# First keys in four loads, first key sketches in one wide buffer, a and b loaded behind the values, and a new order of the opening

## The chip, the cores and the metric

The kernel runs on one core of a Trainium2 chip. The metric is device time in microseconds of one execution; lower is better. The core has five engines that run their own instruction streams and wait for each other through semaphores: PE (matrix multiply, with weight loads shown apart as PEld), DVE (vector), ACT (scalar, with activation functions), POOL (used here for small set-up work) and SP (issues loads and stores). Loads and stores can be issued on SP's queue or on ACT's; in the profile SP's is q1 and ACT's q10, and the packets of both run on 16 DMA engines.

## The reference

Four batches of four heads with 1088 tokens of width 32 go through a linear attention with a polynomial sketch of rank 8, and the result through a dense layer with a rational activation.

```python
def phi(x):                                   # [b, h, s, 32] -> [b, h, s, 64]
    a = np.einsum('rd,bhsd->bhsr', S1, x)
    b = np.einsum('rd,bhsd->bhsr', S2, x)
    return np.einsum('bhsi,bhsj->bhsij', a, b).reshape(*x.shape[:-1], r * r)
q_p, k_p = phi(q), phi(k)
kv = np.einsum('bhsf,bhsd->bhfd', k_p, v)
z = np.sum(k_p, axis=2)
num = np.einsum('bhsf,bhfd->bhsd', q_p, kv)
den = np.einsum('bhsf,bhf->bhs', q_p, z)[..., None] + 1e-06
x = (num / den)                               # -> [4352, 128]
h = x @ w_in                                  # [4352, 2048]
P = a[0] + a[1]*h + a[2]*h**2 + a[3]*h**3
Q = 1.0 + abs(b[0])*abs(h) + abs(b[1])*h**2
return (P / (Q + 1e-06)) @ w_out              # [4352, 128]
```

## The kernel before

**Keys.** Tokens are laid out so that a partition holds 34 tokens of one head (4 heads x 32 groups). They are seen as `NM` = 4 runs m of `NT` = 9 tiles t, of which the last run has only `NL` = 7 (W = 288 floats to a run). DVE transposes blocks of them into `kT` (`kt0` to `kt3`, L250), PE multiplies with the two sketch matrices (`ks`, L256), ACT copies the second half of the sketches out of PSUM (`kc`, L263), DVE forms their outer product with the first half (`kf`, L268), and PE multiplies with the values (`kp`, L297), adding up over all tiles. ACT then copies the sums into `kvz` (`kk`, L307). For the first batch there are three parts of sketches (tiles 0 and 1, 2 and 3, 4 to 8) and four blocks of transposes: kt0 and kt1 take two tiles of all four runs, kt2 tiles 4 to 8 of three runs, kt3 tiles 4 to 6 of the fourth.

**Queries.** For each block of tokens: transpose (`qt`, L320, DVE), sketches (`qs`, L333, PE), copy (`qc`, ACT), features (`qf`, DVE), products with kvz (`qp`, L360, PE), division (`qd`, `qi`, `qx`), transpose back on PE (`qb`) and copy into `xT` (`qk`, L390, ACT). The first two blocks (0 and 1) use a wide PSUM buffer for their sketches. Later blocks of each batch send their sketches through DRAM to spread them over the partitions (class `Spread`).

**The dense layer.** Tokens go in units of 256 or 512. Hidden matmuls (`h`, L446) fill a wide buffer of two PSUM banks, ACT casts it to bfloat16 (`e`, L452), DVE forms the denominator (`u`, `w`, `y`), ACT takes its inverse through a logarithm and an exponential (`ln`, `ex`), DVE forms the numerator's terms (`s`, `m`, `x`, and `pa` on ACT or `pd` on DVE), and PE gathers the output (`G`, L579). The output weights are loaded in two halves (`lw`), scaled by a[0] and a[1] or only cast, and kept in bfloat16 in six pieces (`wo`, L612 to L616; ACT makes 0, 1, 3 and 5, DVE makes 2 and 4).

**Order.** The string `ORDER` is the program's order: each token is a step and an index, and each engine runs its own instructions in that order. Loads are steps too: `lw` output weights, `lq` queries, `lx` input weights, `lk` keys, `lv` values; for index 0, `lq` is the second part of the first batch's queries. `tn` runs matmuls on zeros whose result nobody reads; `TURNS` gives their number: tn:0 has 10, tn:1 and tn:4 have 2 each. `ba` takes the absolute value of b.

**Buffers.** PSUM has two wide buffers (`wide`, 1024 floats, two banks) and four single banks (`bank`). The wide ones serve, in the order of the program, the first keys' sketches, the first two query blocks, and then the hidden matmuls. A new tile takes a buffer whose last reader stands earlier in the order, and its first writer waits for that reader. `kT` has one buffer, features of keys have two, transposed queries (`qT`) two.

**The first loads.** SP issues the sketch matrix S2, the first four tiles of all four runs of keys (256 KB), the first half of the queries, and the values in four loads; ACT issues S1, the rest of the keys (240 and 48 KB), a and b, and loads its activation table. The steps of ORDER follow on SP.

Of the kernel before, what the change touches and what calls it, by code (L numbers as in the profile page):

```python
# [20 lines left out]
ORDER = """
tn:4 tn:0 lw:1 kt0:0 lq:0 kt2:0 lw:0 kt3:0 lx:1 kt1:0 ks0:0 lk:1 qt:0 ks2:0 kc0:0 lx:0 kf0:0 ba:0 qt:1 tn:1 kc2:0 qs:0
kf2:0 qc:0 kp0:0 qf:0 ks1:0 qs:1 kc1:0 kf1:0 qc:1 kp1:0 wo:1 qt:3 kp2:0 qf:1 qt:2 qs:3 kk:0 lq:1 wo:4 lv:1 qp:0 wo:0
qs:2 qd:0 qc:2 qi:0 qx:0 wo:5 qf:2 qb:0 qp:1 qk:0 qc:3 wo:3 h2:0 qd:1 qi:1 qx:1 kt0:1 h3:0 wo:2 e2:0 qt:5 qt:4 qp:2
kt1:1 e3:0 h1:0 pa1:0 u1:0 w1:0 h0:0 y1:0 qd:2 e1:0 qi:2 qx:2 qs:4 e0:0 qb:1 qb:2 qt:6 ks1:1 qk:1 u0:0 qk:2 ln1:0 w0:0
ks0:1 y0:0 h1:1 kc1:1 ex1:0 kf1:1 lk:2 h3:1 lq:2 e1:1 s1:0 kc0:1 h0:1 e3:1 kf0:1 pa0:0 m1:0 h2:1 qf:3 e0:1 x1:0 qp:3
qc:4 e2:1 kt0:2 h0:2 ln0:0 u1:1 kt1:2 h1:2 w1:1 e0:2 ex0:0 y1:1 ks0:2 h2:2 e1:2 s0:0 qd:3 ln0:1 h3:2 qi:3 m0:0 e2:2
lk:3 qx:3 kp1:1 x0:0 e3:2 ex0:1 u1:2 qb:3 lv:2 G0:0 pd0:1 qk:3 w1:2 ln1:1 G1:0 G2:0 qf:4 G3:0 kc0:2 kk:1 y1:2 ex1:1
G4:0 G5:0 kf0:2 qp:4 ln0:2 s0:1 qs:5 G0:1 qd:4 qc:5 qi:4 ex0:2 qt:7 G1:1 qx:4 m0:1 qb:4 ks1:2 qk:4 s1:1 pa1:1 h2:3
s0:2 kc1:2 m1:1 h3:3 e2:3 kf1:2 h1:3 e3:3 st:0 x1:1 ln1:2 qs:7 x0:1 h0:3 e1:3 kt1:3 m0:2 h2:4 e0:3 pd1:2 pa0:2 u1:3  # L30
h3:4 qt:9 w1:3 e2:4 G2:1 ex1:2 x0:2 h0:4 qf:5 e3:4 kp1:2 s1:2 pa0:3 y1:3 h1:4 qc:7 e0:4 m1:2 ln0:3 qp:5 kt0:3 e1:4
G3:1 x1:2 ex0:3 G4:1 m0:3 G5:1 u1:4 ks0:3 qd:5 ln1:3 qi:5 G0:2 w1:4 G1:2 pa1:3 qx:5 G2:2 y1:4 lv:3 qb:5 G3:2 qk:5
ex1:3 h0:5 m1:3 v0:3 kk:2 ln0:4 h2:5 s1:3 e0:5 qs:6 G4:2 qf:7 ex0:4 h1:5 x0:3 qt:8 qc:6 e2:5 s0:4 e1:5 h3:5 pd0:4
# [35 lines left out]
def kernel(  # L69
# [161 lines left out]
    class Keys:  # L231
        def __init__(self, b, k_sb, v_sb, first=False):
            self.b, self.dst, self.k_sb, self.v_sb = b, kvz[b % 2], k_sb, v_sb
            self.take = wide if first else bank
# [16 lines left out]

        def sketches(self, part):
            t0, n = self.PARTS[part]
            ab = self.ab[part] = self.take()[:, 0:n * H * 2 * R].rearrange("p (t h s r) -> p t h s r", h=H, s=2, r=R)
            for t in range(t0, t0 + n):
                nc.tensor.matmul(ab[:, t - t0].rearrange("p h s r -> p (h s r)"),  # L256
                                 lhsT=self.kT[:, t * 128:(t + 1) * 128],
                                 rhs=S12.rearrange("p h s r -> p (h s r)"), start=True, stop=True)
# [450 lines left out]
```

## Time and profile before

| | us |
|---|---|
| median of 3 runs | 274.24 |
| lowest and highest | 274.19, 274.42 |
| time of the profiled execution | 274.34 |
| its span on the core | 272.6 |
| first transpose of keys (L250) starts | 5.84 |
| first sketches of keys (L256) start | 6.34 |
| first hidden matmuls (L446) start | 18.82 |

| stretch, us | PE busy | DVE busy | ACT busy | DMA share |
|---|---|---|---|---|
| 0 to 5.84 | 4.65 | 0.92 | 1.28 | 0.56 |
| 262 to 272.6 | 4.76 | 5.30 | 2.83 | 0.34 |

Busy time is in us; the three stretches between stand with the prediction. The DMA share is the mean busy share of the 16 engines, and it can pass 1 because packets overlap. An instruction's start is in us from the span's start. A wait is named by what ended it. PE's busy time in the first stretch is the matmuls on zeros.

### The profile page before, as it was taken

The page shows a single profiled execution, that of the slowest core. Times are in us where ns is not written, and L with a number is a line of the kernel's source. Part 1 is how long each engine was busy: PE and PEld are TensorE (multiplying, and loading weights), DVE is VectorE, ACT ScalarE, POOL GpSimd, SP SyncE. Part 2 cuts the span into 40 slices and gives each one's busy share as a digit, 9 for nine tenths or more (in the row PEclk, how much of TensorE's full clock was granted, in tenths as well). Part 3 has the DMA queues.
Part 4 walks back from the last instruction along what each step waited for, and adds up shares of the span by engine and source line. Part 5 has one row for each costly group of instructions (what it writes and reads, how often), then busy time and mean ns, then how long its engine had stood idle before and what let it go on. Part 6 is the DMA issues. An engine that isn't in the chain of part 4 may idle for free.

```text
span 272.6 us, 3564 instructions
## 1 busy us (share of the span) xinstructions
PE 258.3 (95%) x1318; PEld 135.4 (50%) x1318; DVE 255.9 (94%) x276; ACT 250.0 (92%) x224; POOL 2.9 (1%) x24
## 2 busy tenths in 40 slices
PE   7989999999999899999999999999999999989591
PEld 3778656963564354535454554434544443434230
DVE  2858999999999999999999999999999999999992
ACT  1377999998999999999999999999999999999980
POOL 4000000000000000000000000000000000000000
PEclk9999999999999999999999999999999999999999
DMA  6992607314025062222304000300126100020005
GB/s 166 294 336 80 204 14 173 111 55 95 2 84 129 14 140 77 73 71 39 96 6 117 11 1 6 120 6 0 23 88 96 20 0 0 0 41 1 0 0 77
DMA packets 30465, 19.53 MB, mean 72 GB/s; under 512 B 20337, under 2 KB 26609, under 8 KB 30449
## 3 DMA queue, kind: packets, MB, share of 16 engines
q1 hardware_dynamic: 28416, 18.87, 26.7%
q10 hardware_dynamic: 2032, 0.45, 0.9%
q8 instruction: 10, 0.16, 0.3%
q14 instruction: 7, 0.05, 0.1%
HBM read 16.16 MB, written 3.15 MB: 71 GB/s over the span
## 4 chain that ended last, share of the span: by engine, by line
PE 37%; ACT 28%; DVE 22%; issue 7%; DMA 2%; SPq 1%; DVEq 0%; ACTq 0%
PE h_ps L446 18%; PE att_ps L579 9%; ACT hh L452 8%; ACT ln L537 8%; ACT r L541 7%; ACT p L532 4%; DVE g L549 4%; DVE s L545 4%; DVE w L486 4%; PE att_ps L360 3%; DVE g L560 3%; DVE w L481 2%; DVE u L475 2%; DMA k_sb<-in_k_dram 2%; PE att_ps L297 1%
## 5 line engine op out<-in xcount | busy, mean ns | idle before, releaser
L446 PE MATMUL h_ps<-xT,w_in_sb 128*128 128x512 f32 (+1 forms) x288 | 125.4, 577 | 1.3 <-ACT hh L452 1.1
L446 PEld LDWEIGHTS h_ps<-xT,w_in_sb 128*128 128x128 f32 x288 | 52.2, 190 | 55.9 <-issue 40.5
L452 ACT CAST hh<-h_ps 128x1024 bf16<-128x1024 f32 x68 | 68.3, 1025 | 3.4 <-PE h_ps L446 2.9
L541 ACT ACTIVATE r<-ln 128x2048 bf16<-128x2048 f32 (+1 forms) x35 | 66.0, 1886 | 0.3
L537 ACT ACTIVATE ln<-w 128x2048 f32<-128x2048 bf16 (+1 forms) x35 | 66.0, 1885 | 0.2
L579 PEld LDWEIGHTS <-w_out 128*128 128x128 bf16 x412 | 39.9, 98 | 52.8 <-issue 18.7
L532 ACT ACTIVATE p<-hh,a_sb 128x2048 bf16<-128x2048 bf16 (+1 forms) x23 | 46.7, 2036 | 0.1
L545 DVE TENSOR_TENSOR s<-hh,r 128x2048 bf16<-128x2048 bf16 (+2 forms) x33 | 40.7, 1241 | 0.2
L486 DVE TENSOR_TENSOR w<-w,u 128x4096 bf16<-128x4096 bf16 (+2 forms) x22 | 39.5, 1795 | 0.1
L579 PE MATMUL att_ps<-g,w_out 128*128 128x512 bf16 (+1 forms) x144 | 34.9, 367 | 4.0 <-DVE g L560 3.8
L579 PE MATMUL att_ps<-r,w_out 128*128 128x512 bf16 (+1 forms) x144 | 34.5, 367 | 0.8 <-ACT r L541 0.8
L549 DVE TENSOR_TENSOR g<-hh,s 128x2048 bf16<-128x2048 bf16 (+1 forms) x30 | 35.1, 1172 | 0.0
L560 DVE TENSOR_TENSOR g<-g,p 128x2048 bf16<-128x2048 bf16 (+1 forms) x30 | 34.8, 1173 | 0.0
L579 PE MATMUL att_ps<-s,w_out 128*128 128x512 bf16 (+1 forms) x124 | 30.0, 365 | 0.0
L481 DVE TENSOR_SCALAR w<-u,b_abs 128x4096 bf16<-128x4096 bf16 (+2 forms) x22 | 23.8, 1090 | 0.1
L475 DVE TENSOR_SCALAR u<-hh 128x4096 uint16<-128x4096 uint16 (+2 forms) x22 | 21.3, 970 | 0.6 <-ACT hh L452 0.2
L360 PEld LDWEIGHTS att_ps<-kvz,q_pT 128*128 128x128 f32 x144 | 17.6, 191 | 5.0 <-DVE q_pT L424 1.1
L360 PE MATMUL att_ps<-kvz,q_pT 128*128 128x66 f32 x144 | 17.9, 273 | 0.9 <-DVE q_pT L352 0.5
L297 PEld LDWEIGHTS att_ps<-v_sb,k_p 128*64 128x64 f32 (+1 forms) x288 | 8.8, 138 | 2.6 <-issue 1.8
L527 DVE TENSOR_SCALAR p<-hh,a_sb 128x2048 bf16<-128x2048 bf16 x12 | 9.6, 804 | 0.0
L297 PE MATMUL att_ps<-v_sb,k_p 128*64 128x64 f32 (+1 forms) x288 | 9.5, 224 | 0.0
L424 DVE TENSOR_TENSOR q_pT<-a_all,b_all 128x768 f32<-128x768 f32 (+1 forms) x10 | 8.9, 895 | 0.0
(60 smaller groups left out, 134.9 us busy)
## 6 DMA issues: line engine op xcount, KB each, us to landing
a_all<-sk_d SPq DMA_DIRECT2D x6, 384.0 KB
b_all<-sk_d SPq DMA_DIRECT2D x12, 192.0 KB
v_sb<-in_v_dram SPq DMA_DIRECT2D x12, 144.0 KB
k_sb<-in_k_dram SPq DMA_DIRECT2D x3, 544.0 KB
q_sb<-in_q_dram SPq DMA_DIRECT2D x3, 544.0 KB
a_all<-sk_d SPq DMA_DIRECT2D x4, 320.0 KB
b_all<-sk_d SPq DMA_DIRECT2D x8, 160.0 KB
out_dram<-out_sb SPq DMA_DIRECT2D x18, 64.0 KB
```

Source lines behind the costliest of these rows:

```text
L360: nc.tensor.matmul(self.nd[:, o:o + 2 * KW], lhsT=self.q_p[:, c, x:x + 128], rhs=kvz[self.b % 2][:, c, :], start=True, stop=True)
L446: nc.tensor.matmul(t[:, x * tl:(x + 1) * tl], lhsT=w_in_sb[:, f * 128:(f + 1) * 128], rhs=xT[:, t0:t0 + tl], start=True, stop=True)
L452: nc.scalar.copy(out=live[i]["hh"][:, part * PW:(part + 1) * PW], in_=live[i]["h", part])
L481: nc.vector.tensor_scalar(out=t[:, c], in0=live[i]["u"][:, c], scalar1=ab1, scalar2=ab0, op0=AX.mult, op1=AX.add)
L486: nc.vector.tensor_mul(out=t[:, c], in0=t[:, c], in1=live[i]["u"][:, c])
L532: nc.scalar.activation(out=part_of(i, "p", h), in_=hh, func=ACT.Identity, scale=a3, bias=a2)
L537: nc.scalar.activation(out=t, in_=live[i]["w"][:, span(h)], func=ACT.Ln, bias=1.0 + 1e-6)
L541: nc.scalar.activation(out=part_of(i, "r", h), in_=live[i]["ln"], func=ACT.Exp, scale=-1.0)
L545: nc.vector.tensor_mul(out=part_of(i, "s", h), in0=hh, in1=part_of(i, "r", h))
L549: nc.vector.tensor_mul(out=part_of(i, "g", h), in0=hh, in1=part_of(i, "p" if horner(i, first(h)) else "s", h))
L560: nc.vector.tensor_mul(out=g, in0=g, in1=part_of(i, "s" if horner(i, first(h)) else "p", h))
L579: nc.tensor.matmul(outs[t0][:, :tl], lhsT=w_sb[y][:, f0 + x, :], rhs=part_of(i, key, h)[:, c:c + tl], start=done[0] == 0, stop=done[0] == ...
```

## The change

Computation and instructions of the compute engines are the same; only loads, buffers and order differ.

- The first batch's keys come in four loads. For the first four tiles, and then for tiles 4 to 8, SP's queue takes runs 0 and 1 and ACT's queue runs 2 and 3. The last load is rectangular, so it also reads two tokens past the end of the fourth run (into padding that nothing reads). Before, it was one load on SP and two on ACT.
- a and b are loaded on SP, behind the values, not on ACT.
- All three parts of the first key sketches lie in one wide buffer, at columns 0, 128 and 512; before, each part took a wide buffer of its own.
- ORDER is another permutation of the same 725 steps. In the opening: all 14 matmuls on zeros stand before the first sketches (tn:1 was between ks2 and qs0); PE's order is ks0, ks1, qs0, ks2, kp0, qs1 where it was ks0, ks2, tn:1, qs0, kp0, ks1, qs1; lx:0 stands before lk:1; ba stands behind kk; the pieces wo change places; in the second batch's start DVE runs kt1:1, kt0:1, qt:6, qt:4 and later qt:5, where it ran kt0:1, wo:2, qt:5, qt:4, kt1:1 and later qt:6. Further on some neighbours swap places, the last of them at step 545.
- `LX`, which nothing reads, goes from 2 to 3.

```diff
-    nc.sync.dma_start(out=k0.rearrange("p (m x) -> p m x", m=NM)[:, :, 0:4 * D],
-                      in_=bass.AP(tensor=k.tensor, offset=k.offset, ap=[[S * D // 32, 128], [W, NM], [1, 4 * D]]))
-    nc.scalar.dma_start(out=k0[:, 0:km].rearrange("p (m x) -> p m x", m=NM - 1)[:, :, 4 * D:],
-                        in_=k0_src[:, 0:km].rearrange("p (m x) -> p m x", m=NM - 1)[:, :, 4 * D:])
-    nc.scalar.dma_start(out=k0[:, km + 4 * D:S], in_=k0_src[:, km + 4 * D:S])
+    half, row = NM // 2, S * D // 32
+    for t0, t1 in ((0, 4), (4, NT)):
+        for x, queue in enumerate((nc.sync, nc.scalar)):
+            at = x * half * W + t0 * D
+            queue.dma_start(out=k0.rearrange("p (m x) -> p m x", m=NM)[:, x * half:(x + 1) * half, t0 * D:t1 * D],
+                            in_=bass.AP(tensor=k.tensor, offset=k.offset + at, ap=[[row, 128], [W, half], [1, (t1 - t0) * D]]))
...
-    nc.scalar.dma_start(out=a_sb, in_=bass.AP(tensor=moe_a.tensor, offset=moe_a.offset,
-                                              ap=[[0, 128]] + list(moe_a.ap)))
-    nc.scalar.dma_start(out=b_sb, in_=bass.AP(tensor=moe_b.tensor, offset=moe_b.offset,
-                                              ap=[[0, 128]] + list(moe_b.ap)))
     nc.scalar.preload_act_table_set("natural_log_exp_and_others")
     load_v(0)
+    nc.sync.dma_start(out=a_sb, in_=bass.AP(tensor=moe_a.tensor, offset=moe_a.offset,
+                                            ap=[[0, 128]] + list(moe_a.ap)))
+    nc.sync.dma_start(out=b_sb, in_=bass.AP(tensor=moe_b.tensor, offset=moe_b.offset,
+                                            ap=[[0, 128]] + list(moe_b.ap)))
...
         def sketches(self, part):
             t0, n = self.PARTS[part]
-            ab = self.ab[part] = self.take()[:, 0:n * H * 2 * R].rearrange("p (t h s r) -> p t h s r", h=H, s=2, r=R)
+            if self.first:
+                if not self.ab:
+                    self.all = wide()
+                at = (0, 128, 512)[part]
+            else:
+                self.all, at = bank(), 0
+            ab = self.ab[part] = self.all[:, at:at + n * H * 2 * R].rearrange("p (t h s r) -> p t h s r", h=H, s=2, r=R)
```

The opening of ORDER, before and after:

```diff
-tn:4 tn:0 lw:1 kt0:0 lq:0 kt2:0 lw:0 kt3:0 lx:1 kt1:0 ks0:0 lk:1 qt:0 ks2:0 kc0:0 lx:0 kf0:0 ba:0 qt:1 tn:1 kc2:0 qs:0
-kf2:0 qc:0 kp0:0 qf:0 ks1:0 qs:1 kc1:0 kf1:0 qc:1 kp1:0 wo:1 qt:3 kp2:0 qf:1 qt:2 qs:3 kk:0 lq:1 wo:4 lv:1 qp:0 wo:0
-qs:2 qd:0 qc:2 qi:0 qx:0 wo:5 qf:2 qb:0 qp:1 qk:0 qc:3 wo:3 h2:0 qd:1 qi:1 qx:1 kt0:1 h3:0 wo:2 e2:0 qt:5 qt:4 qp:2
+tn:1 tn:0 kt0:0 kt1:0 kt3:0 lw:1 kt2:0 tn:4 lq:0 ks0:0 qt:0 lw:0 ks1:0 qt:1 kc0:0 lx:1 qs:0 kf0:0 kc1:0 lx:0 kf1:0
+lk:1 qc:0 ks2:0 qf:0 kp0:0 kc2:0 qs:1 kf2:0 qc:1 kp1:0 wo:1 qf:1 kp2:0 qt:3 qt:2 qs:3 kk:0 lq:1 qp:0 lv:1 ba:0 wo:3
+qs:2 qd:0 qc:2 qi:0 qx:0 wo:0 qf:2 qb:0 qp:1 wo:4 qk:0 qc:3 wo:5 h2:0 qd:1 qi:1 wo:2 qx:1 h3:0 e2:0 kt1:1 kt0:1 qp:2
```

More of the change, by code (lines that the diff above doesn't have):

```diff
@@ L21 @@
 ORDER = """
-tn:4 tn:0 lw:1 kt0:0 lq:0 kt2:0 lw:0 kt3:0 lx:1 kt1:0 ks0:0 lk:1 qt:0 ks2:0 kc0:0 lx:0 kf0:0 ba:0 qt:1 tn:1 kc2:0 qs:0
-kf2:0 qc:0 kp0:0 qf:0 ks1:0 qs:1 kc1:0 kf1:0 qc:1 kp1:0 wo:1 qt:3 kp2:0 qf:1 qt:2 qs:3 kk:0 lq:1 wo:4 lv:1 qp:0 wo:0
-qs:2 qd:0 qc:2 qi:0 qx:0 wo:5 qf:2 qb:0 qp:1 qk:0 qc:3 wo:3 h2:0 qd:1 qi:1 qx:1 kt0:1 h3:0 wo:2 e2:0 qt:5 qt:4 qp:2
-kt1:1 e3:0 h1:0 pa1:0 u1:0 w1:0 h0:0 y1:0 qd:2 e1:0 qi:2 qx:2 qs:4 e0:0 qb:1 qb:2 qt:6 ks1:1 qk:1 u0:0 qk:2 ln1:0 w0:0
-ks0:1 y0:0 h1:1 kc1:1 ex1:0 kf1:1 lk:2 h3:1 lq:2 e1:1 s1:0 kc0:1 h0:1 e3:1 kf0:1 pa0:0 m1:0 h2:1 qf:3 e0:1 x1:0 qp:3
@@ L27 @@
[L27 to L31, printed above, removed]
@@ L32 @@
-G3:1 x1:2 ex0:3 G4:1 m0:3 G5:1 u1:4 ks0:3 qd:5 ln1:3 qi:5 G0:2 w1:4 G1:2 pa1:3 qx:5 G2:2 y1:4 lv:3 qb:5 G3:2 qk:5
-ex1:3 h0:5 m1:3 v0:3 kk:2 ln0:4 h2:5 s1:3 e0:5 qs:6 G4:2 qf:7 ex0:4 h1:5 x0:3 qt:8 qc:6 e2:5 s0:4 e1:5 h3:5 pd0:4
+tn:1 tn:0 kt0:0 kt1:0 kt3:0 lw:1 kt2:0 tn:4 lq:0 ks0:0 qt:0 lw:0 ks1:0 qt:1 kc0:0 lx:1 qs:0 kf0:0 kc1:0 lx:0 kf1:0
+lk:1 qc:0 ks2:0 qf:0 kp0:0 kc2:0 qs:1 kf2:0 qc:1 kp1:0 wo:1 qf:1 kp2:0 qt:3 qt:2 qs:3 kk:0 lq:1 qp:0 lv:1 ba:0 wo:3
+qs:2 qd:0 qc:2 qi:0 qx:0 wo:0 qf:2 qb:0 qp:1 wo:4 qk:0 qc:3 wo:5 h2:0 qd:1 qi:1 wo:2 qx:1 h3:0 e2:0 kt1:1 kt0:1 qp:2
@@ new lines @@
+qt:6 e3:0 qt:4 h1:0 pa1:0 u1:0 w1:0 h0:0 y1:0 qd:2 e1:0 qi:2 qx:2 qs:4 e0:0 qb:2 qb:1 qt:5 ks1:1 qk:1 u0:0 qk:2 ln1:0
+w0:0 h1:1 y0:0 kc1:1 ex1:0 ks0:1 kf1:1 h2:1 lk:2 e1:1 s1:0 lq:2 kc0:1 h0:1 kf0:1 e2:1 pa0:0 m1:0 h3:1 qf:3 e0:1 x1:0
+qp:3 qc:4 e3:1 kt0:2 h1:2 ln0:0 u1:1 kt1:2 h3:2 w1:1 e1:2 qd:3 ex0:0 qi:3 y1:1 h0:2 e3:2 G0:0 s0:0 e0:2 h2:2 ln1:1
+qx:3 m0:0 lk:3 kp1:1 x0:0 e2:2 ex1:1 u1:2 qb:3 lv:2 ks0:2 pd0:1 qk:3 w1:2 ln0:1 G1:0 G2:0 qf:4 G3:0 ex0:1 y1:2 G4:0
+G5:0 kc0:2 kk:1 kf0:2 qp:4 ln0:2 s0:1 qs:5 G0:1 qd:4 qc:5 qi:4 ex0:2 qt:7 G1:1 qx:4 s1:1 qb:4 ks1:2 qk:4 m0:1 pa1:1
@@ L34 @@
+h2:3 s0:2 kc1:2 m1:1 h3:3 e2:3 kf1:2 h1:3 e3:3 kt1:3 st:0 ln1:2 x1:1 h0:3 x0:1 e1:3 qs:7 pd1:2 e0:3 h2:4 m0:2 pa0:2
+u1:3 h3:4 qt:9 e2:4 x0:2 G2:1 ex1:2 w1:3 h0:4 qf:5 e3:4 kp1:2 s1:2 pa0:3 y1:3 qc:7 e0:4 h1:4 kk:2 m1:2 ln0:3 qp:5
+kt0:3 e1:4 x1:2 G3:1 ex0:3 G4:1 m0:3 G5:1 u1:4 qd:5 G0:2 ln1:3 qi:5 ks0:3 w1:4 G1:2 pa1:3 qx:5 lv:3 G2:2 y1:4 qb:5
+G3:2 qk:5 ex1:3 h0:5 m1:3 v0:3 ln0:4 h2:5 s1:3 e0:5 qs:6 G4:2 qf:7 ex0:4 h1:5 x0:3 qt:8 qc:6 e2:5 s0:4 e1:5 h3:5 pd0:4
 pa1:4 m0:4 h1:6 v1:3 e3:5 x0:4 G5:2 ln1:4 u1:5 h3:6 st:2 e1:6 w1:5 qp:7 ex1:4 x1:3 h0:6 e3:6 y1:5 qd:7 pa0:5 lq:3 G0:3
@@ L38 @@
 y1:7 kc1:3 qp:8 ex1:6 h2:8 pd1:6 kc0:3 e3:8 s1:6 ln0:7 h0:8 kf0:3 e2:8 m1:6 G2:5 ex0:7 G3:5 x0:6 G4:5 kf1:3 qd:8 e0:8
-qs:10 G5:5 ln1:7 qi:8 u1:8 kp1:3 qx:8 pa0:7 w1:8 qb:8 G0:6 qf:9 qk:8 y1:8 qc:10 h3:9 ex1:7 s0:7 h2:9 e3:9 s1:7 ln0:8
+qs:10 G5:5 ln1:7 qi:8 u1:8 kp1:3 qx:8 pa0:7 w1:8 qb:8 qf:9 G0:6 qk:8 y1:8 qc:10 h3:9 ex1:7 s0:7 h2:9 e3:9 s1:7 ln0:8
 h0:9 m0:7 e2:9 x1:6 G2:6 e0:9 h1:10 x0:7 ex0:8 pd1:7 h1:9 m1:7 pa0:8 s0:8 G3:6 e1:9 u1:9 G0:7 qt:11 ln1:8 qp:9 qt:12
@@ L45 @@
 G4:8 ex1:10 G5:8 G1:9 m0:10 ln0:11 G2:9 qf:11 h2:12 s1:10 ex0:11 x0:10 h3:12 pa1:10 m1:10 qs:12 G3:9 s0:11 e2:12 G4:9
-pd0:11 qc:12 ln1:11 qp:11 m0:11 x1:10 G5:9 e3:12 G0:10 x0:11 qd:11 ex1:11 G1:10 qi:11 u1:12 G2:10 pa1:11 G3:10 qx:11
+pd0:11 qc:12 ln1:11 qp:11 m0:11 x1:10 G5:9 e3:12 G0:10 x0:11 qd:11 ex1:11 G1:10 qi:11 u1:12 G2:10 pa1:11 qx:11 G3:10
 w1:12 qb:11 G4:10 qk:11 s1:11 pa0:12 h1:13 y1:12 h2:13 e1:13 m1:11 ln0:12 h3:13 st:6 x1:11 ex0:12 G5:10 qf:12 st:10
@@ L61 @@
 QUARTER = (16,)
-LX = 2
+LX = 3
 WIDE_S = (3, 5)
@@ L134 @@
     k0 = io.tile([128, NM * W], FP, name="k_sb", bufs=1)
-    k0_src = k[0].rearrange("h (g j) d -> (h g) (j d)", g=32)
-    km = (NM - 1) * W
     s_raw = []
@@ L233, in __init__ @@
             self.b, self.dst, self.k_sb, self.v_sb = b, kvz[b % 2], k_sb, v_sb
-            self.take = wide if first else bank
             self.first = first
```

## The prediction

> **What bounds the kernel.** I read the page first, then busy time by stretch, the chain of waits, and the opening instruction by instruction.
>
> ```profile
> PE 258.3 (95%) x1318; PEld 135.4 (50%) x1318; DVE 255.9 (94%) x276; ACT 250.0 (92%) x224; POOL 2.9 (1%) x24
> ```
>
> Three engines are near full, so the place where they are not decides. Busy time by stretch (start and end, length, then PE, weight loads, DVE, ACT, POOL):
>
> ```profile
> 5.84:18.82 12.98, 11.66 (x139) 8.89 (x138) 9.22 (x19) 6.74 (x17) 0.00 (x0) 1.00 1.05 326
> 18.82:28.00 9.18, 9.18 (x52) 7.79 (x51) 7.55 (x15) 7.35 (x9) 0.00 (x0) 1.00 0.46 113
> 28.00:262.00 234.00, 228.06 (x1101) 115.37 (x1100) 232.90 (x231) 231.80 (x197) 0.00 (x0) 1.00 0.22 55
> ```
>
> From 28 to 262 us DVE idles 234.00 - 232.90 = 1.1 us in all. Both kernels give DVE the same instructions, so what the opening takes from the moment when DVE becomes gapless comes off the end nearly whole, and a DVE wait added later costs its full length. Profiled time is 274.34 (span 272.6 and 1.7 around it); the median of the runs is 274.24, 0.1 less.
>
> The chain of waits through the opening (start, length, what):
>
> ```profile
> 1.47 4.34 DMA k_sb<-in_k_dram
> ...
> 5.84 1.17 DVE kT L250 x3
> ...
> 7.06 1.33 PE h_ps L256 x10
> 8.38 0.43 PE att_ps L169 x2
> 8.82 1.09 PE h_ps L333 x8
> ...
> 11.29 1.13 PE h_ps L333 x8
> 12.43 1.69 PE att_ps L297 x52
> ```
>
> Keys land, DVE transposes, and then PE is the bound: five-tile sketches (ks2), two idle matmuls (tn:1), first query sketches (qs0), a wait for qf0, qs1, and the products that give kvz.
>
> **The loads.** The two queues' traffic, in 3.4 to 3.8 us and then 3.8 to 4.2 (packets, MB, share of 16 engines):
>
> ```profile
> q10 hardware_dynamic: 222, 0.14, 111.2%
> ```
> ```profile
> q1 hardware_dynamic: 218, 0.11, 94.2%
> ```
>
> ACT's 240 KB, the late tokens, crosses first (q10); SP's first tokens (q1) begin only at 3.8, though SP issues them at 1.47. After the change each queue's first load is 128 KB of first tokens. Summed over such windows 0.26 MB has crossed by about 3.9 us and 0.59 MB by 5.0. SP's third value load left at 4.34, which the waits put on a load of keys: data gone by 3.9 was seen about 0.4 later. Estimate: first tokens 4.6 (bounds 4.3, ACT's old landing, and 5.84, today's); all keys, 0.64 MB with the sketch weights and 45 KB of padding that the wider loads read, 5.6 (5.2 to 6.2). Then the queries:
>
> ```profile
> 6.87 0.37 SPq L637 DMA_DIRECT2D q_sb<-in_q_dram  x1
> ```
>
> This issue waited for the first query load, so that landed at 6.87. Padding adds 45 KB at some 0.3 MB/us, 0.15 us; a and b, which held 12 to 16% of the engines from 5.4 to 6.6 with almost no bytes (q10's share in such windows), now come behind the values. I keep 6.87 (6.5 to 7.5).
>
> Issues seem to wait for the load eight places earlier (third value load on ACT's keys, L637 on the queries). By that count a and b wait for keys on SP and lw:1 leaves at about 6.2 as now; lq:0, lw:0 and lx:1 behind it shift by 0 to 0.5 us. The rings are full from 6 to 19 us (share 1.0 to 1.1), which hides that. Without this cover wo:1, and kk behind it on ACT, would slip as much; lq:0, behind lw:1 in the ring, is already read at 11.99, and wo:1 now starts at 12.25. ba moves behind kk: nothing until w0 and w1 (24.36) reads it; its 0.20 us lies where ACT waits for qs2.
>
> **The opening, step by step.** DVE: kt0 and kt1 0.37 each (start to start), kt3 0.23, kt2 0.6: done by 6.4 if all keys are there at 5.6; qt:0 6.87 to 7.27, qt:1 to 7.7.
>
> PE has 14 idle matmuls ahead instead of 12.
>
> ```profile
> 5.43 0.11 PEld L169 LDWEIGHTS <-idle 128*128 128x128 bf16 x1 [0.28 <-issue]
> ```
>
> Weight loads before this one took 0.15 and came 0.43 apart; from here the array runs at double pace, and the two cost 0.43 (row at 8.38). The twelve end at 6.03, so ks0 starts at 6.4 against 6.34: **earlier keys do not move PE's start.** What moves is behind it: ks0 and ks1, eight at 0.133 (1.33 for ten), to 7.46; qs0 then, not after ks2 and tn:1: 7.46 against 8.75. qs0 1.09 to 8.55; ks2 1.33 to 9.88; kp0 0.6 (9.81 to 10.42) to 10.48. qs1 needs qf0: qc0 0.59 and qf0 0.69 end at 9.95, covered by kp0. So **qs1 starts at 10.5 against 11.29**. kc2 ends at 10.25; kf2 takes the feature buffer that kp0 frees, 10.6 to 12.1, when kp1 ends; kp1 and kp2 1.69, to 13.3 against 14.12. ACT: qc1 to 12.25, wo:1 1.15 to 13.4, kk there against 14.19: 0.8 earlier. If keys and queries take their late bounds, qs0 starts at 7.95 and 0.5 of this goes; early bounds give nothing more, since PE has no hole.
>
> From kk on the old spacing holds; wo:0 (1.15) stands ahead of qk0 where wo:5 (1.06) stood: hidden matmuls begin at 18.1 against 18.82, **0.7 earlier**.
>
> One wide buffer: are sketch parts serialised? Bank 0 holds parts 0 and 1, so kc0 may have to wait for ks1 (0.5 us); kf0 stands behind qt:1 till 7.7, which covers it. No row shows this; bounds 0 and 0.3 on kf1, covered by kp0 too.
>
> **The second batch.**
>
> ```profile
> 22.15 1.04 DVE L320 STREAM_TRANSPOSE qT<-q_sb 128x384 f32<-128x384 f32 x2 [0.73 <-DMA q_sb<-in_q_dram]
> ...
> 23.62 0.69 DVE L475 TENSOR_SCALAR u<-hh 128x2048 uint16<-128x2048 uint16 x1
> ...
> 27.41 0.51 DVE L320 STREAM_TRANSPOSE qT<-q_sb 128x320 f32<-128x320 f32 x1 [0.35 <-PE att_ps L401]
> ```
>
> lq:1's landing at 22.15 doesn't move: it sits behind full rings. So the stall goes here: DVE reaches it at 21.0 and waits 1.1 us, not 0.73. Then two transposes (1.0) and u1:0 at 23.2, not behind kt1:1 as now: 0.4 earlier. The work up to the third transpose takes 3.44: 26.65; PE's qs4, 0.7 earlier, frees its buffer at 26.7 against 27.41, and u0:0 follows 0.7 earlier. lk:1 goes behind lx:0 in the queue: 512 KB at 0.41 MB/us, 1.25 us; by bytes it lands near 17, and kt1:1 wants it at 19.5.
>
> **Sum:** no instruction saved; 0.8 from ks2 and tn:1 leaving the front, less 0.1 for wo:0: 274.34 - 0.7 = **273.6**.
>
> **Rivals.** (A) *More:* qk0 and lq:1 give nothing back, and DVE loses some of its 1.1 us of later waits through the reordered tail of the opening: 0.8 + 0.3 to 0.5, 273.1. For it: four weighted copies change places; against: rows above.
>
> (B) *The loads gain nothing.* First tokens land at 5.84 as now, since two queues are not more engines: kt0, kt1, kt3, kt2 (1.57) end at 7.41, qt:0 at 7.8, qs0 at 7.85: 0.4 of the gain goes, 274.0. Against: q10's bytes now precede q1's, and they change hands. The Trainium skill ("DMA: Bandwidth & Descriptors", Issuing engines are not separate DMA queues) speaks for it: loads issued from several engines share the same 16 and save only issue time. The two rows agree that the engines were full with one queue at a time; what they leave open to the change is order, and the skill's rule doesn't forbid that.
>
> (C) *Slower:* the second batch arrives later. DVE's kt1:1, kt0:1, qt:6 stand in front of u1:0. Bytes put lq:1 at 18.2, yet it landed at 22.15: something holds a load for 4 us (an instruction packet, q8, runs at 16 to 17 us). If that lag takes hold of lk:1 too, or of lq:1 by more, u1:0 starts at landing + 1.05, and from 22.6 on the gain is gone. At 23.5 it starts at 24.55: 0.9 late, **275.2**. For it: lk:1 is later in the queue, and SP has two more small loads; against: the same bytes.
>
> (D) *It doesn't do what it says:* qs1 takes the keys' buffer and must wait for kf2. At 12.1 instead of 11.29 it costs 0.8: 275.1. Against: buffers go by release, not in turn: qb0 ran at 16.82 while the bank next in turn was read at 18.65 (L407).
>
> (E) *The array stays slow for all 14 idle matmuls:* 1.19 + 14 x 0.425 = 7.14, so ks0 starts 0.75 later and the gain is gone: 274.3. Against: the runs of before differ by 0.2 us only. The Trainium skill ("TensorE: Matmul & The Clock Gate", Part 1: the HAM clock gate) has the clock double after a free-running window of activity, so that the number of slow matmuls differs from run to run; this trace shows eleven slow ones of twelve, in one run.
>
> **Chances.** Forecast 0.48 (own range 273.3 to 273.9), A 0.17, B 0.11, C 0.18, D 0.04, E 0.02. 0.2% is 0.55 us, about what a measurement of this kernel tells from no change: under 273.7 is faster. The forecast's range lies there by three quarters or more (0.38, same 0.10), all of A (0.17), a little of B (0.03, same 0.08), none of C and D, and E is no change: **faster 0.58, same 0.20, slower 0.22.** Range 272.9 to 274.9: the unknown landings (0.5), A below and the lesser half of C above.
>
> **What would show it.** Right: first kT transpose before 5; ks0 at 6.4; qs0 near 7.5 and qs1 near 10.5 with no PE gap between; kvz at 13.4; hidden matmuls at 18.1; DVE waiting about 1.1 us for q_sb at 22; the 28 to 262 stretch as gapless. Wrong: qs1 at 12 (D), qs0 at 7.85 (B), u1:0 after 23.6 (C), or DVE idle above 2 us after 28.

## The result, and the profile after

The changed kernel takes **275.06 us** (median of 6 runs, 274.95 to 275.7) against 274.27 for the kernel before in the same session (6 runs, 274.19 to 274.5): ratio 1.003, 95% interval 1.002 to 1.0041. It is slower by 0.8 us; 273.6 was forecast. Its profiled execution took 275.07 us, span 273.3, against 274.34 and 272.6: 0.7 us longer, and the traces say where. One execution each of experiments 1, 10 and 11 below took about 278 us, and their ratios leave it out.

The three engines' busy time did not change, as the page's first part shows:

```profile
PE 258.1 (94%) x1318; PEld 135.8 (50%) x1318; DVE 255.7 (94%) x276; ACT 250.1 (92%) x224; POOL 2.9 (1%) x24
```

Nor did the gapless stretch. Busy time by stretch, with the columns as in the prediction:

```profile
5.84:18.82 12.98, 10.91 (x136) 8.72 (x134) 8.42 (x17) 6.25 (x15) 0.00 (x0) 1.00 1.07 322
18.82:28.00 9.18, 9.16 (x51) 7.64 (x50) 7.06 (x15) 7.25 (x10) 0.00 (x0) 1.00 0.56 124
28.00:262.00 234.00, 228.19 (x1103) 115.77 (x1102) 232.82 (x231) 232.09 (x198) 0.00 (x0) 1.00 0.22 55
```

DVE idles 234.00 - 232.82 = 1.2 us between 28 and 262 us, as before (1.1). Between 5.84 and 18.82 every engine does less than it did (DVE 8.42 against 9.22, ACT 6.25 against 6.74), but this row alone shows no loss: DVE did 0.77 us more ahead of it (1.69 against 0.92 up to 5.84), since its transposes now start at 5.07, and some other work moved behind it. The opening's chain of waits tells more (start, length, what):

```profile
2.84 4.36 DMA q_sb<-in_q_dram
...
7.23 0.77 DVE qT L324 x2
8.00 0.58 DVE k_p L272
8.58 0.02 issue
8.61 0.22 ACT b_sk L267
8.83 0.02 issue
8.85 0.70 DVE k_p L272
9.55 0.04 issue
9.60 1.33 PE h_ps L260 x10
10.92 0.62 PE att_ps L301 x16
11.54 1.06 PE h_ps L337 x8
12.60 1.89 PE att_ps L301 x52
...
19.29 3.72 PE h_ps L450 x16
```

Before, the chain went from the landing of the first keys through PE's sketches. Now it starts with the queries, and then goes through something new: DVE's first key product (kf0), ACT's copy of the second part (kc1), DVE's second product (kf1), and only then PE's ten sketches of part 2 (ks2, at 9.60). The same instructions in the timeline (start, length, engine, line, what; in brackets the idle time just before and what ended it):

```profile
8.61 0.21 ACT L267 COPY b_sk<-h_ps 128x64 f32<-128x64 f32 x1 [1.28 <-DVE k_p L272]
8.85 0.69 DVE L272 TENSOR_TENSOR k_p<-h_ps,b_sk 128x512 f32<-128x512 f32 x1 [0.28 <-ACT b_sk L267]
...
9.60 1.33 PE L260 MATMUL h_ps<-S,kT 128*128 128x64 f32 x10 [0.64 <-DVE k_p L272]
...
10.85 0.69 PE L301 MATMUL att_ps<-v_sb,k_p 128*64 128x64 f32 x16
...
11.47 1.14 PE L337 MATMUL h_ps<-qT,SAB 64*128 64x256 f32 x8
11.66 1.49 DVE L272 TENSOR_TENSOR k_p<-h_ps,b_sk 128x1280 f32<-128x1280 f32 x1 [1.36 <-PE att_ps L301]
```

kf1 needs kc1's copy, but the other two waits are not for data: kc1 reads part 1's sketches and kf0 those of part 0, and ks2 writes part 2, at column 512, which kf1 doesn't read. What they share is the one wide buffer. PE has nothing else for 0.64 us, and kp0, qs1, kf2 and all behind them slip: qs1 starts at 11.47 (before 11.29), the hidden matmuls at 19.29 (before 18.82).

From there the delay goes to the end. DVE instructions paired with the same ones before start 0.47 us later near 25 us, 0.62 near 32, 0.56 near 72, and 0.39 at each one sampled from 104 us to the last transpose of outputs (267.65 against 267.26). The other 0.3 us lie behind that transpose: from its start to the span's end 272.6 - 267.26 = 5.3 us before, 273.3 - 267.65 = 5.6 after.

### The profile page after: what moved, and what is told of

Same layout as the page of the kernel before. It is cut to its first block, busy times and chain, and to the rows that moved or that the text cites. A ratio compares the mean times of both kernels' runs of the same rounds, so it can differ in the third digit from the quotient of the medians.

```text
span 273.3 us, 3567 instructions
## 1 busy us (share of the span) xinstructions
PE 258.1 (94%) x1318; PEld 135.8 (50%) x1318; DVE 255.7 (94%) x276; ACT 250.1 (92%) x224; POOL 2.9 (1%) x24
## 4 chain that ended last, share of the span: by engine, by line
DVE 44%; PE 22%; ACT 20%; issue 8%; DMA 2%; SPq 2%; DVEq 0%; ACTq 0%
PE h_ps L450 10%; DVE g L553 8%; DVE s L549 7%; DVE w L490 7%; PE att_ps L583 7%; ACT ln L541 6%; DVE g L564 6%; ACT r L545 5%; ACT hh L456 5%; DVE w L485 4%; DVE u L479 3%; PE att_ps L364 3%; ACT p L536 2%; DMA q_sb<-in_q_dram 2%; DVE q_pT L428 1%
```

## The experiments

Each median is compared with runs of the kernel before on the same chip in the same batch; below, "before" in a run means these. A shift is a DVE instruction's start in the profile minus that of the same instruction in the kernel before; plus is later. One profile is one execution, and shifts hold for that one.

**1. Two banks.** Parts 0 and 1 share a single bank, part 2 has one of its own.

```diff
-            if self.first:
-                if not self.ab:
-                    self.all = wide()
-                at = (0, 128, 512)[part]
+            if self.first and part == 1:
+                at = 128
             else:
                 self.all, at = bank(), 0
```

> The changed kernel, but the first keys' sketch parts 0 and 1 lie in one single PSUM bank and part 2 in another, as separate tiles, and not in one wide buffer. Theory (the shared buffer makes ks2 wait on PE for kf1, which reads the same buffer): ks2 starts when qs0 ends, at about 9.0 instead of 9.60; qs1 at about 10.9 instead of 11.47; hidden matmuls at about 18.7 instead of 19.29; time about 274.5. kc1 still waits for kf0 (same bank). Rival (the late query load alone, 7.22 against 6.87, shifts the whole opening): qs1 stays at 11.4 or later, hidden matmuls at 19.3, time 275.0.

Measured 274.64 against 274.38, ratio 1.0009 (1.0 to 1.0018). Its timeline:

```profile
8.71 0.21 ACT L265 COPY b_sk<-att_ps 128x64 f32<-128x64 f32 x1 [1.74 <-DVE k_p L270]
8.96 0.69 DVE L270 TENSOR_TENSOR k_p<-att_ps,b_sk 128x512 f32<-128x512 f32 x1 [0.28 <-ACT b_sk L265]
8.99 1.33 PE L258 MATMUL att_ps<-S,kT 128*128 128x64 f32 x10
...
10.87 1.13 PE L335 MATMUL h_ps<-qT,SAB 64*128 64x256 f32 x8
...
18.67 3.50 PE L448 MATMUL h_ps<-xT,w_in_sb 128*128 128x256 f32 x15
```

kc1 still waits for kf0, which reads the same bank, but ks2 no longer waits for kf1: it follows qs0 at 8.99, while kf1 is only starting. qs1 comes 0.6 earlier than in the changed kernel (11.47), and so do the hidden matmuls (18.67 against 19.29), although the queries landed no earlier. That is the delay of the opening, and it is more than the whole 0.47 us that it lost against before.

**2. Own banks.** Each part takes a single bank.

```diff
-            if self.first:
-                if not self.ab:
-                    self.all = wide()
-                at = (0, 128, 512)[part]
-            else:
-                self.all, at = bank(), 0
+            self.all, at = bank(), 0
```

> The changed kernel, but each of the three first key sketch parts has a single bank of its own. Theory: kc0 no longer waits for ks1 and kc1 no longer for kf0, so kc1 runs at about 7.2 instead of 8.61, qc0 at about 8.95 unchanged, kf1 follows kf0 without a gap, and ks2 follows qs0; hidden matmuls at about 18.6, time 274.3 to 274.5. If the late queries are the whole cause: 19.3 and 275.0. If the wait moves to the feature buffer that kp0 frees, kf2 starts at about 11.0 and kp2 ends at about 13.9 in spite of the earlier qs1.

Measured 274.45, ratio 1.0001 (0.9984 to 1.0019). In its timeline kc1's wait for kf0 is gone as well:

```profile
7.83 0.21 ACT L262 COPY b_sk<-att_ps 128x64 f32<-128x64 f32 x1 [0.23 <-PE att_ps L255]
...
9.02 1.33 PE L255 MATMUL att_ps<-S,kT 128*128 128x64 f32 x10
...
10.89 1.13 PE L332 MATMUL h_ps<-qT,SAB 64*128 64x256 f32 x8
```

qs1 is where experiment 1 had it (10.87). So kc1's wait shows no cost of its own; what costs is that ks2 stands behind it.

The two waits can be told apart by a rule. The Trainium skill ("PSUM — Partial Sum Buffer", PSUM bank collisions raise a hardware error) has it that two engines must be kept apart by bank and group of 32 partitions, two readers too, and not by address. The traces agree for kc1, which waits for kf0 where both parts lie in one bank (1.28 us in the changed kernel, 1.74 in experiment 1) and not where each has its own (experiment 2); but parts in one bank were always in one buffer too, so these runs don't tell the bank from the buffer. The rule does not ask for the wait of ks2, whose columns begin a second bank. That wait went when part 2 got a buffer of its own; what in the shared buffer asks for it was not tested further.

**3. The loads alone.** The kernel before with the four key loads of the changed one; a and b stay on ACT.

```diff
-    nc.sync.dma_start(out=k0.rearrange("p (m x) -> p m x", m=NM)[:, :, 0:4 * D],
...
+    for t0, t1 in ((0, 4), (4, NT)):
+        for x, queue in enumerate((nc.sync, nc.scalar)):
...
```

> The kernel before with the four key loads alone; a and b stay on ACT behind the key loads, the order and the buffers are the old ones. Theory (the loads are nearly neutral, the buffer and the order do the harm): first transpose at about 5.0, but kt2 follows kt0 in the old order and waits for all keys until 6.0, so ks0 starts near 5.9 and the five-tile sketches at about 6.9; qs0 0.1 to 0.3 earlier than 8.75; time 274.0 to 274.3. Rival (the loads harm, since queries land later): queries land at 7.2 and qs0 starts after 8.75, time 274.5 or more.

Measured 274.40, ratio 1.0002 (0.9994 to 1.0011). Its timeline:

```profile
5.34 0.45 DVE L251 STREAM_TRANSPOSE kT<-k_sb 128x256 f32<-128x256 f32 x1 [1.55 <-DMA k_sb<-in_k_dram]
...
6.41 1.16 DVE L251 STREAM_TRANSPOSE kT<-k_sb 128x480 f32<-128x480 f32 x3 [0.62 <-DMA k_sb<-in_k_dram]
...
7.31 1.33 PE L257 MATMUL h_ps<-S,kT 128*128 128x64 f32 x10 [0.80 <-DVE kT L251]
```

The first tokens are there 0.5 earlier (5.34 against 5.84), the late ones later, and the old order wants those second: PE waits 0.80 us for them. qs0 starts 0.25 later than before. This shift of 0.25 near 19 us is 0.25, 0.23, 0.23 and 0.24 near 25, 72, 104 and 213 us and 0.21 at the last transpose. So DVE's work does pass an opening shift on to the end, in the direction of a loss. The theory's earlier qs0 and its 274.0 to 274.3 were missed. The rival's late queries (they landed at 7.38) and late qs0 (9.00) came, but qs0 stood behind ks2 and tn:1 and not behind the queries, and the time is below its 274.5.

**4. Three small loads more on SP**, in the kernel before, near 235 us, read by nothing.

```diff
+    spare = consts.tile([1, 4], FP, name="spare")
...
             store(i)
+            if i == 6:
+                for _ in range(3):
+                    nc.sync.dma_start(out=spare, in_=moe_a[None, :])
```

> The kernel before with three more tiny loads (16 bytes each) on SP near 235 us, into a buffer that nothing reads. The changed kernel has three more instructions on SP, and after its last store has landed it takes 0.5 us more to its end than before (stores 0.40 later, end 0.91 later). Theory (SP's longer program costs this at its end, through fetching instructions or one more closing wait): time 274.5 to 274.8 with the last store's landing unchanged. Rival (an accident of this one profile, or set by something else): 274.2 to 274.3.

Measured 274.17, ratio 0.9992 (0.9983 to 1.0). The longer program on SP costs nothing here: from the last transpose to the end 5.2 us. The idea that SP's two loads more explain the 0.3 us at the end by their number fell.

**5. The order alone.** The new ORDER with own banks, the old key loads, and a and b on ACT. Against experiment 2:

```diff
-    for t0, t1 in ((0, 4), (4, NT)):
-        for x, queue in enumerate((nc.sync, nc.scalar)):
...
+    nc.sync.dma_start(out=k0.rearrange("p (m x) -> p m x", m=NM)[:, :, 0:4 * D],
...
+    nc.scalar.dma_start(out=a_sb, in_=bass.AP(tensor=moe_a.tensor, offset=moe_a.offset,
...
```

> The changed kernel with the key loads of before, a and b back on ACT, and a single PSUM bank for each of the three first key sketch parts: the new order alone. Theory (the order is worth something, the shared buffer took it back, and the queries' landing gates qs0 in either set of loads): first transpose at 5.84, all keys and the queries by 6.87, kt0, kt1, kt3, kt2 end at 7.4, qs0 at 7.85, ks2 to 10.3, hidden matmuls near 18.6; time 274.2 to 274.5. If the four loads were needed for it, qs0 comes after 8.2 and hidden matmuls after 18.9.

Measured 274.24 against 274.47, ratio 0.9992 (0.9983 to 1.0001). In its timeline ks2 follows qs0, and DVE waits for the second batch's queries:

```profile
8.17 1.13 PE L333 MATMUL h_ps<-qT,SAB 64*128 64x256 f32 x8 [0.79 <-DVE qT L320]
...
9.24 1.33 PE L256 MATMUL att_ps<-S,kT 128*128 128x64 f32 x10
```
```profile
22.31 0.97 DVE L320 STREAM_TRANSPOSE qT<-q_sb 128x320 f32<-128x320 f32 x2 [0.73 <-DMA q_sb<-in_q_dram]
```

Here the queries landed only at 7.56, and the order brings the hidden matmuls no earlier than before (18.93). The shift is +0.11 at 25 us, +0.26 at 32, +0.19 at 72, -0.01 at 104. The fall of about 0.2 between 72 and 104 us is in every profile with this order, and a rise of 0.10 to 0.15 between 25 and 32 in most of them: the reordered middle gives back what the order lost there, and little more. The time is the theory's; qs0 at 8.17 and the hidden matmuls at 18.93 lie at the edge of the other case, but they follow the late queries, and the four loads don't bring those earlier (7.2 to 7.8 in the changed kernel and experiments 2 and 11).

**6. Queries before the late keys.** Own banks, SP's load of the queries ahead of its second load of keys, the first transpose of queries ahead of kt3 and kt2.

```diff
     for t0, t1 in ((0, 4), (4, NT)):
...
+        if not t0:
+            nc.sync.dma_start(out=q0[:, 0:512], in_=q0_src[:, 0:512])
...
-tn:1 tn:0 kt0:0 kt1:0 kt3:0 lw:1 kt2:0 tn:4 lq:0 ks0:0 qt:0 lw:0 ks1:0 qt:1 kc0:0 lx:1 qs:0 kf0:0 kc1:0 lx:0 kf1:0
+tn:1 tn:0 kt0:0 kt1:0 qt:0 lw:1 kt3:0 kt2:0 tn:4 lq:0 ks0:0 lw:0 ks1:0 qt:1 kc0:0 lx:1 qs:0 kf0:0 kc1:0 lx:0 kf1:0
```

> The changed kernel with a bank for each part, and SP issues the first half of the queries between its two key loads; in the order qt:0 stands before kt3 and kt2. Theory (after the buffer, the queries' landing at 7.2 is what the opening waits for): queries land at 6.2 to 6.5, qs0 starts at 6.7 to 7.0 when the array is warm (up to 7.8 where all 14 idle matmuls run slow), ks2 waits for kt2 at about 7.7, hidden matmuls at about 18.2 if the values (landed at 9.71) let kp0 start at 9.8; time 274.0 to 274.3. Rival (DVE's wait for lq:1 near 22 takes all of it): DVE waits 1.8 us there, u1:0 starts near 23.5 as before, time 274.4.

Measured 274.89 (273.82 to 275.39), ratio 1.0012 (1.0002 to 1.0021). The profiled execution is the fastest of the twelve, 273.82:

```profile
6.12 0.45 DVE L320 STREAM_TRANSPOSE qT<-q_sb 128x256 f32<-128x256 f32 x1 [0.33 <-DMA q_sb<-in_q_dram]
...
8.36 1.33 PE L256 MATMUL att_ps<-S,kT 128*128 128x64 f32 x10
```
```profile
22.12 0.97 DVE L320 STREAM_TRANSPOSE qT<-q_sb 128x320 f32<-128x320 f32 x2 [1.34 <-DMA q_sb<-in_q_dram]
```

Queries at 6.1 bring the hidden matmuls to 18.13, where the prediction had put them, and the shift is -0.78 near 19 us. DVE then stands 1.34 us at the second batch's queries, and -0.65 is left at 25 us; -0.54 at 32 and, after the 0.2 that the middle gives back, -0.82 at the last transpose. So a gain of the opening passes to the end too, less 0.1 at that stall. But most runs are a microsecond slower than this one, and the median missed both times named; no profile shows the slower ones.

**7. The same with the second batch's transpose moved.** `qt:6` behind `qx:2`, so that DVE does not stand before that landing.

```diff
-qt:6 e3:0 qt:4 h1:0 pa1:0 u1:0 w1:0 h0:0 y1:0 qd:2 e1:0 qi:2 qx:2 qs:4 e0:0 qb:2 qb:1 qt:5 ks1:1 qk:1 u0:0 qk:2 ln1:0
+e3:0 qt:4 h1:0 pa1:0 u1:0 w1:0 h0:0 y1:0 qd:2 e1:0 qi:2 qx:2 qt:6 qs:4 e0:0 qb:2 qb:1 qt:5 ks1:1 qk:1 u0:0 qk:2 ln1:0
```

> The same, with qt:6 moved behind qx:2 in the order, so that only one transpose of the second batch's queries stands before u1:0 on DVE. Theory (lq:1's landing near 22 with two transposes behind it is the wall): u1:0 starts 0.4 to 0.5 earlier than with qt:6 in front, at the end of e3:0 (near 23.0); time 273.6 to 274.0. Rival: the wall is elsewhere (ACT's casts), and the time is that of the kernel with qt:6 in front.

Measured 274.64 (273.89 to 275.95), ratio 1.0008 (0.9997 to 1.0019). It doesn't decide: the profiled execution is the slowest, with queries at 8.0, the late keys at 8.6 and 8.9, and still a wait for the second batch's queries:

```profile
8.03 0.45 DVE L320 STREAM_TRANSPOSE qT<-q_sb 128x256 f32<-128x256 f32 x1 [2.08 <-DMA q_sb<-in_q_dram]
```
```profile
24.74 0.58 DVE L320 STREAM_TRANSPOSE qT<-q_sb 128x384 f32<-128x384 f32 x1 [1.30 <-DMA q_sb<-in_q_dram]
```

What it does show is the size of the scatter: the same load order landed the queries at 6.1 and at 8.0, and the last transpose came 2.1 us apart.

**8. The changed kernel with the three small loads of experiment 4.**

```diff
+            if i == 6:
+                for _ in range(3):
+                    nc.sync.dma_start(out=spare, in_=moe_a[None, :])
```

> The changed kernel with three more tiny loads on SP near 235 us, as was done to the kernel before. There the gap of 0.4 us between two of SP's closing instructions fell while the last store was still landing, and the time was 0.2 us less. Theory (a stall of some 0.4 us sits at a fixed place of SP's program near its end, and the changed kernel's three more instructions on SP move it to behind the last store's landing): time 274.6 to 274.8, against 275.06; DVE's last transpose unmoved (267.65). Rival (the end is not set by SP's count): 275.0 to 275.1.

Measured 275.08 against 274.47, ratio 1.0025 (1.0014 to 1.0035). From the last transpose to the end 5.4 us, not 5.6, but the shift at that transpose is +0.78 here, and the median does not fall: the theory's 274.6 to 274.8 was missed and the rival's 275.0 to 275.1 came. ks2 waits as ever, 0.65 us for kf1.

**9. The shared buffer alone.** Experiment 5 with the wide buffer of the change.

```diff
-            self.all, at = bank(), 0
+            if self.first:
+                if not self.ab:
+                    self.all = wide()
+                at = (0, 128, 512)[part]
+            else:
+                self.all, at = bank(), 0
```

> The new order with the old key loads and a and b on ACT's queue (as in the run with the order alone), but with the three first sketches in one wide buffer as in the changed kernel. Theory A (the shared buffer is what loses: TensorE's third group of ten sketches must wait for VectorE's reading of the second part, though they use other columns): the third group waits for the second key product, first hidden activation some 0.6 us later than the 18.93 of the order alone, so near 19.5; VectorE's shift against before near +0.6 at 32 us and +0.3 at the last transpose; time 274.6 to 275.0. Theory B (the buffer is harmless, the new loads and the two small ones on SP lose): third group right after the query sketch, hidden at 18.9 to 19.0, time 274.2 to 274.4.

Measured 274.73 against 274.49, ratio 1.0009 (0.9999 to 1.0018); experiment 5 had 0.9992. The wait is back:

```profile
9.01 0.21 ACT L268 COPY b_sk<-h_ps 128x64 f32<-128x64 f32 x1 [0.76 <-DVE k_p L273]
...
10.01 1.33 PE L261 MATMUL h_ps<-S,kT 128*128 128x64 f32 x10 [0.93 <-DVE k_p L273]
```

The hidden matmuls start at 19.70, 0.8 later than in experiment 5, although the first transpose of queries ran 0.35 earlier (7.23 against 7.58). Some of it is the late start of the first sketches (7.01), which kc0, kf0, kc1 and kf1 hand on to ks2. The time is A's; the shifts, +1.03 at 32 us and +0.79 at the last transpose, go the way A said and further. B's 18.9 to 19.0 fell, and so did its time.

**10. The changed kernel with a and b on ACT**, ahead of the values, as before.

```diff
-    nc.sync.dma_start(out=a_sb, in_=bass.AP(tensor=moe_a.tensor, offset=moe_a.offset,
...
+    nc.scalar.dma_start(out=a_sb, in_=bass.AP(tensor=moe_a.tensor, offset=moe_a.offset,
...
     nc.scalar.preload_act_table_set("natural_log_exp_and_others")
     load_v(0)
```

> The changed kernel with a and b left on ACT's queue, ahead of the first values as before; shared buffer, new order and four key loads stay. Theory A (shared buffer): no relief, third group of sketches still waits for the second key product, hidden at 19.2 to 19.5, time 274.8 to 275.1. Theory C (a and b on SP cost, in SP's closing instructions or in the landing of the first queries): the stretch from the last transpose's start to the end falls from 5.65 to near 5.3, time 274.5 to 274.7.

Measured 275.21 (274.69 to 278.26), ratio 1.0033 (1.0012 to 1.0054). ks2 waits 0.69 us for kf1 and the hidden matmuls start at 19.37, as A said; the time lies 0.1 above A's. C's stretch at the end is right and its time is wrong. The last transposes of the changed kernel and of this one, with the spans:

```profile
core 0 of [0], span 273.3 us
...
267.65 0.72 DVE L592 STREAM_TRANSPOSE out_sb<-att_ps 128x512 f32<-128x512 f32 x1 [0.68 <-PE att_ps L583]
```
```profile
core 0 of [0], span 272.9 us
...
267.68 0.72 DVE L592 STREAM_TRANSPOSE out_sb<-att_ps 128x512 f32<-128x512 f32 x1 [0.68 <-PE att_ps L583]
```

273.3 - 267.65 = 5.6 against 272.9 - 267.68 = 5.2. But the median is no lower than the changed kernel's.

**11. Own banks, and a and b on ACT**: of the change, the order and the four loads alone. The diff of experiment 10, and this:

```diff
-            if self.first:
...
+            self.all, at = bank(), 0
```

> The changed kernel with every part of the sketches in its own bank and a and b on ACT's queue: new order and four key loads alone. Theory A (shared buffer is the loss): hidden at 18.6 to 18.9, shift of VectorE's last transpose -0.3 to -0.1, time 274.0 to 274.4. If the four key loads cost something of their own beside the new order (they gave +0.24 us with the old order): hidden near 19.1, time 274.4 to 274.6.

Measured 274.39, ratio 0.9996 (0.9986 to 1.0007). In its profile the queries landed at 7.85 and the hidden matmuls started at 19.20, the shift at the last transpose is +0.25. By the profile that is the other case named (near 19.1), by the time (274.39) it lies where both meet. The hidden matmuls follow the first transpose of queries by 11.35 us, exactly as in experiment 2 (7.37 and 18.72), so what was late was the queries. From the last transpose to the end 5.2 us.

**12. The order alone with the three small loads**, that is experiments 5 and 4 together.

```diff
+            if i == 6:
+                for _ in range(3):
+                    nc.sync.dma_start(out=spare, in_=moe_a[None, :])
```

> The order alone (own banks, old key loads, a and b on ACT) with three 16-byte loads more on SP near 235 us, which nothing reads. Theory S (a stall of 0.2 to 0.3 us among SP's closing instructions depends on how many it has; three more hid it in the kernel before and partly in the changed one): stretch from the last transpose's start to the end near 5.25, as with the order alone (5.28), so no further gain: 274.1 to 274.3. Rival (the three loads give 0.2 us whatever the kernel): 274.0 to 274.1.

Measured **274.14** (273.32 to 274.37) against 274.49, ratio 0.9975 (0.9965 to 0.9986); the medians alone give 0.9987. It is the only kernel here whose interval lies below 1. Its profiled execution is its fastest:

```profile
6.31 1.00 PE L257 MATMUL att_ps<-S,kT 128*128 128x64 f32 x8
6.63 0.73 DVE L321 STREAM_TRANSPOSE qT<-q_sb 128x256 f32<-128x256 f32 x2
...
8.30 1.33 PE L257 MATMUL att_ps<-S,kT 128*128 128x64 f32 x10
```

With the queries at hand at 6.63 and ks2 at 8.30, qs1 starts at 10.18 and the hidden matmuls at 18.00. From the last transpose to the end it takes 5.2 us, as without the loads, so theory S's stretch and time hold; why the ratio is lower than experiment 5's 0.9992 (0.9983 to 1.0001), which was taken on another chip, is not shown.

Put in a square, the order being new in all four and a and b on ACT:

| ratio to before | each part its own bank | one wide buffer |
|---|---|---|
| old key loads | 0.9992 (0.9983 to 1.0001) | 1.0009 (0.9999 to 1.0018) |
| four key loads | 0.9996 (0.9986 to 1.0007) | 1.0033 (1.0012 to 1.0054) |

The wide buffer costs 0.2% with the old loads and 0.4% with the new ones, 0.5 to 1 us. With a and b on SP it is 1.0001 (0.9984 to 1.0019) and 1.003 (1.002 to 1.0041). The four loads bring nothing in either column.

## Why the prediction was wrong, step by step

**The step that failed** is "One wide buffer: are sketch parts serialised?", with its bounds of 0 and 0.3 on kf1, "covered by kp0 too". It asked only whether kc0 waits for ks1 in bank 0, and had no term for part 2 in the second bank. The waits that came were others: kc1 for kf0, so kf1 began only at 8.85, 0.28 behind kf0 and so within the bound; and ks2 for kf1, 0.64 us on PE, which the step did not list. kp0 could not cover this, since kp0 stands behind ks2 on PE. Taking the shared buffer away put ks2 behind qs0 and the hidden matmuls 0.62 earlier (experiment 1); putting it into a kernel without it brought the wait back (experiment 9).

The rest, against its own numbers:

- **DVE passes the shift to the end:** right, for losses (experiment 3) and gains (experiments 6 and 12: -0.91 near 19 us and -0.96 at the last transpose in the latter).
- **The loads:** first tokens were to land at 4.6; kt0 started at 5.07. The reason for the direction was right, the size not. In the windows of 3.4 to 3.8 us the queues now carry (packets, MB, share of 16 engines)

```profile
q1 hardware_dynamic: 95, 0.05, 61.8%
q10 hardware_dynamic: 21, 0.01, 19.5%
```

0.06 MB where q10 alone carried 0.14, in rows of four tiles instead of five, and the engines are not full. The estimate by summed bytes took the old rate. Its 45 KB of padding was wrong too: the four loads are 128, 128, 160 and 160 KB for 544 KB of keys, which leaves 32 KB, by the prediction's own 0.3 MB/us a difference of 0.04 us.
- **Queries at 6.87:** SP's issue that waits for them, and the transpose,

```profile
7.22 0.33 SPq L641 DMA_DIRECT2D q_sb<-in_q_dram  x1
7.23 0.77 DVE L324 STREAM_TRANSPOSE qT<-q_sb 128x256 f32<-128x256 f32 x2 [0.52 <-DMA q_sb<-in_q_dram]
```

say 7.2, within the bounds of 6.5 to 7.5. But "PE has no hole" held no longer: queries, not PE, now bound the opening, and each tenth counts. With own banks qs1 starts 3.5 us after the first transpose of queries in four of the profiles (7.37 and 10.89, 7.58 and 11.11, 7.85 and 11.38, 6.63 and 10.18): 6.87 would have given 10.4, the forecast.
- **PE's start:** 6.4 forecast, 6.08 measured, because the idle matmuls went to double pace earlier (5.00 against 5.43); it did not matter, since qs0 waited 0.74 for the queries.
- **qs0 at 7.46, qs1 at 10.5, kvz at 13.4, hidden matmuls at 18.1:** 7.82, 11.47, 14.57, 19.29. The 1.2 us of the last are 0.62 for the buffer, 0.35 for the queries, and 0.2 between qs1 and kvz (3.1 measured, 2.9 forecast).
- **The second batch:** the stall of 1.1 us at the queries of 22 us did not come, since the opening was late and the queries landed at 21.7:

```profile
21.87 0.93 DVE L324 STREAM_TRANSPOSE qT<-q_sb 128x320 f32<-128x320 f32 x2
24.10 0.70 DVE L479 TENSOR_SCALAR u<-hh 128x2048 uint16<-128x2048 uint16 x1 [1.30 <-ACT hh L456]
```

u1:0 waited for ACT's cast, which waits for the late hidden matmuls. With own banks the stall came as forecast, 1.2 to 1.4 us, where the queries of the first batch landed by 7.4 (experiments 1, 2, 6 and 12), and 0.7 where they landed later (5 and 11).
- **The end** had no term: 0.3 us came there.

The sum: forecast -0.7, measured +0.7 in the span. Of the 1.4 between them, 1.2 stand at the hidden matmuls as above, 0.1 came back by the last transpose, and 0.3 were added behind it. The buffer alone does not make up the forecast's miss: without it (experiment 2) the kernel is as fast as before and no faster. There the last transpose came 0.24 us earlier and the end took 0.24 longer. The forecast's path, with its hidden matmuls at 18.1, came only where the queries landed by 6.2 (experiments 6 and 12, profiles of 273.82 and 273.32).

**Rivals.** A did not come: DVE idles 1.2 us between 28 and 262 us, not less than before. D named a keys' buffer as the place and 275.1 as the time, which is what came, but by luck: its mechanism, qs1 waiting for kf2, did not come, and qs1 followed kp0 without a hole. C's 275.2 lies as near, by luck as well: its late landing did not come. B's qs0 at 7.85 came out for another reason, the queries. E's slow pace for all 14 idle matmuls came in several runs (first sketches at 6.79, 6.86, 7.01 and 7.13 in experiments 2, 8, 9 and 11), but in experiments 2, 8 and 11 qs0 waited for the queries.

**What stays open:** why the changed kernel's median does not fall when the 0.3 us at the end go (experiment 10), and how the runs that were not profiled differ, those of experiment 6 above all (up to 275.39 behind a profile of 273.82). A kernel with the shared buffer and another place for ks2 in the order was not tried.

## What to carry to other kernels

When several steps come to share one buffer, list for each writer every reader of the whole buffer that stands ahead of it in the program, and for each reader the other engines' readers of its bank, and look up where the writer stands on its own engine: a wait between parts that share no data cost 0.6 us here because the next matmuls stood behind it. Shortening an opening pays only up to the next landing, so name the landing that binds next, and how far it scatters from run to run, before counting the gain.
